# The first block of every other AFNO chunk gets a buffer of its own, and its transfer out is issued in two parts

## The chip, the cores and the metric

The program runs on one core of one Trainium2 chip, as one launch. The metric is device time in microseconds (us), lower is better, given as the median of several runs. A hardware profile of one execution on the same core goes with it. In it PE is TensorE, DVE VectorE, ACT ScalarE, POOL GpSimd and SP SyncE, which here only issues transfers. PSUM is the memory that matmuls write to, SBUF the on-chip working memory; a transfer is a DMA, and it "lands" when its semaphore tells that all of its data has arrived.

## The reference, cut to what matters

One row of conditioning `c` gives six vectors (shift, scale and gate for each of two sublayers). The first sublayer is a spectral block (AFNO) on a sequence of 4096 rows of 640 columns, the second a gated feed-forward block.

```python
mod = (_silu(c) @ w_mod).reshape(c.shape[0], 6, 1, -1)
sa, ca, ga, sb, cb, gb = (mod[:, 0], mod[:, 1], mod[:, 2], mod[:, 3], mod[:, 4], mod[:, 5])
h = _layernorm(x) * (1 + ca) + sa
x = x + ga * _A_ref(h, A_w1, A_b1, A_w2, A_b2)     # spectral block
h = _layernorm(x) * (1 + cb) + sb
x = x + gb * _B_ref(h, B_w_gate, B_w_up, B_w_down) # silu(h Wg) * (h Wu) Wd, F = 1728

# _A_ref: rfft over the rows, then per frequency and per block of 160 of the 640 columns:
hr = relu(zr @ w1[0] - zi @ w1[1] + b1[0]);  hi = relu(zi @ w1[0] + zr @ w1[1] + b1[1])
or_ = hr @ w2[0] - hi @ w2[1] + b2[0];       oi_ = hi @ w2[0] + hr @ w2[1] + b2[1]
# soft threshold: sign(v) * max(|v| - 0.01, 0) for or_ and oi_, then irfft
```

## The kernel before, in words

The program has three parts. A first stage normalizes `x`, takes a short Fourier transform along one factor of the row index and writes the result to scratch memory. The AFNO loop, which the change touches, does the rest of the forward transform, the two small layers, the soft threshold and the first half of the inverse transform. The feed-forward part ends the inverse transform and does the second sublayer; its instructions are put in order by a planner in the code, and the change does not touch it.

**The AFNO loop.** The frequencies are done in 8 chunks (`ch`) of 256 (258 in chunk 4), the 640 columns in 4 blocks (`b`) of 160. One step `p = 4 * ch + b` is one chunk and one block. The loop over `p` writes all engines' instructions in this order, and each engine runs its own in that order (the scheduler is off there). A step is software-pipelined: step `p` does layer 1 of block `p` (`stage_l1`), the transform of a later chunk's columns (`stage_b`, `evac_b`, `evac_rh`, `evac_rl`), layer 2 of block `p - 1` (`stage_l2`), the inverse transform of a piece that is seven steps old (`stage_i`), and, between them, pieces of the soft threshold (`shrink_parts`, `shrink`, `shrink_high`, `shrink_low`).

**Where layer 2 goes.** `stage_l2` makes, for each half `q` of the chunk's 256 frequencies, a PSUM tile `pc` of 128 frequencies by 2 x 160 values (real, imaginary). DVE adds the bias (L731) and writes the result into columns `160 * b` of a tile `tt` of 128 x 2 x 640. There are two `tt` buffers in all, one for each `q`. So block 0 of a chunk writes into the buffers that still hold the chunk before.

**The moves.** After the last block of chunk `ch - 1` is written, at the end of step `p = 4 * ch`, `move_x` puts eight transfers on the SP queue (L745): for each of four pieces `i` (quarters of the chunk's frequencies) two, one for the real and one for the imaginary half, from 64 partitions of `tt` into 64 partitions of a tile `xx` of 128 x 640. Block 0 of chunk `ch` is written in step `4 * ch + 1`; the semaphores make it wait until the moves that read its buffer have landed.

**The threshold.** ACT computes two relus of `xx` (`shrink_parts`, L751 into `cl`, L752 in place) in step `4 * ch + 1 + i` for piece `i` of chunk `ch - 1`, behind that step's layer-1 evacuations; DVE subtracts them at the start of the next step (L757). Then ACT and DVE split the result in a high and a low part (L766, L771) for the inverse matmuls `pi` (L782 to L784), which ACT evacuates (L785). In step `p` ACT's queue goes on, behind `shrink_parts`, with the next step's evacuations of layer 1 (`h`, L682 and L683; `u` first part, L696), and DVE's with the second part of `u` (L697). The second `pi` of a step takes the PSUM buffer that `u` was evacuated from.

**The conditioning vectors.** Beside this, four of the six vectors are computed on DVE, 20 rows of `w_mod` in 20 steps: `mod_load` fetches 128 x 640 numbers into the tile `wm` through the SP queue (L553), and `mod_add` multiplies and adds them into `acc` (L558 for the first of a vector, L560 for the others). `wm` has one buffer, so a load waits for the `mod_add` before it. In the steps that write block 0, a `mod_add` stands right behind the two bias additions (step 5) or behind one L771 more (steps 9, 13, 21, 25).

**What sets the order.** SP issues its transfers strictly in the order written, each after the semaphores that it waits for; a transfer also waits for the one eight transfers before it, since eight semaphores are used in turn. Nothing else is issued on SP while one waits.

At the end of the loop the first rows of the feed-forward part are prepared in three tiles, of which the third takes the place of `wm` (line 1009), and the feed-forward part begins with loads `cr` (L1504) of the AFNO result.

Of the kernel before, what the change touches and what calls it, by code (L numbers as in the profile page):

```python
# [13 lines left out]
P = 128  # L14
D = 640
# [158 lines left out]
def body(tc, x, w1, b1, w2, b2, wg, wu, wd, c, wm, k_fa, k_tb, k_tx, k_bm, k_bx, k_ga, k_ge, k_id, out, dbg=None):  # L174
# [27 lines left out]
    with ExitStack() as top:  # L202
# [35 lines left out]
        with ExitStack() as af:  # L238
# [292 lines left out]

            acc = p2.tile([P, D], F32, name="acc")
# [16 lines left out]
            wmts = {}  # L549

            def mod_load(m, k):
                wmts[m, k] = p2.tile([P, D], F32, tag="wm", bufs=1, name=f"wm{m}_{k}")
                nc.sync.dma_start(wmts[m, k], wm[:, m, k, :])  # L553

            def mod_add(m, k):
                wmt = wmts[m, k]
                if k == 0:
                    dve.tensor_scalar(acc, wmt, sc[:, 0:1], None, op0=OP.mult)  # L558
                else:
                    dve.scalar_tensor_tensor(acc, wmt, sc[:, k:k + 1], acc, op0=OP.mult, op1=OP.add)  # L560
                if (m, k) == (0, 4):
                    remainders(acc, wx)
# [44 lines left out]
            tts = {}  # L607

# [104 lines left out]
            def stage_l2(ch, b, then=()):  # L713
                h0, h1, r2, _ = hss[ch, b]
                de = slice(160 * b, 160 * b + 160)
                for q in range(3 if ch == CE else 2):
# [3 lines left out]
                    if b == 0 and q < 2:  # L720
                        tts[ch, q] = p2.tile([P, 2, D], F32, tag="tt", bufs=2, name=f"tt{ch}_{q}")
# [8 lines left out]
                    if q < 2:  # L730
                        dve.tensor_tensor(tts[ch, q][:, :, de], pc[:, :320].rearrange("p (r e) -> p r e", r=2),  # L731
                                          b2t[:, :, b, :], op=OP.add)
                        if then:
                            then[q]()
                    else:

                        dve.tensor_tensor(tts[ch, 0][0:1, 1, de], pc[0:1, :160], b2t[0:1, 0, b, :], op=OP.add)
# [3 lines left out]
            def move_x(ch, i):  # L741
                q, h = i // 2, i % 2
                xx = p2.tile([P, D], F32, tag="xx", bufs=5, name=f"xx{ch}_{i}")
                for r in range(2):
                    nc.sync.dma_start(xx[64 * r:64 * r + 64, :], tts[ch, q][64 * h:64 * h + 64, r, :])  # L745
                xxs[ch, i] = xx

# [100 lines left out]
            for p in range(LAST + 1):  # L848
# [35 lines left out]
                if b == 0 and ch:  # L884
                    for i in range(4):
                        move_x(ch - 1, i)
                if p == 0:
# [9 lines left out]
                for f, *a in mods.get(p, ()):  # L897
                    f(*a)
                if p == LAST - 4:
# [108 lines left out]
            for i in range(3):  # L1008
                xns[0].append(p2.tile([P, D], F32, tag="co" if i < 2 else "wm", bufs=2 if i < 2 else 1, name=f"xn0_{i}"))
# [1202 lines left out]
```

## Time and profile before

| | us |
|---|---|
| median of 3 runs | 1473.19 (1470.07 to 1473.38) |
| time of the profiled execution | 1472.98 |
| span of the profiled execution | 1471.2 |
| AFNO loop, first layer-2 result to the last `xx` move | 72.9 to about 277 |
| DVE's waits for the moves before it writes `tt` | 12.0 in 6 waits |
| mean granted clock of PE | 0.991 |

A row of the chain or of the groups names the engine, the line of the code, the operation and the tiles (out<-in). In a timeline row the first number is the start in us from the span's start, the second the duration, and what stands in brackets is the idle time just before the row and the instruction that ended it. A row `PE pi L782 <- DVE u L697: 1.9, 2, 1.2` of the table of waits says that PE, before line 782, stood idle for 1.9 us in 2 waits, the longest 1.2, and that line 697 on DVE ended them. Matmul busy time is pipelined time, so PE at 97% does not mean that PE is at its peak; it does mean that there is little room between matmuls.

### The profile page before, as it was taken

Reading aid. Unit: us, or ns where it says so; the run is one execution under the profiler, and the core shown is the slowest. Engines: PE = TensorE matmul, PEld = TensorE weight load, DVE = VectorE, ACT = ScalarE, POOL = GpSimd, SP = SyncE. Lnnn points to the kernel's source line nnn. Section 1 sums busy time; section 2 is a strip of 40 time slices with the busy share of each in tenths; the row PEclk is TensorE's granted clock in tenths of the full one; section 3 lists DMA queues with packets and bytes.
Section 4 is the critical chain, followed back from the end, with each engine's and each line's share of the span. In section 5 each row is a group of like instructions: output and inputs, shape, how many; then the busy total and the mean of one; then the engine's idle time right before and its main releaser. Section 6 shows DMA issues by size and latency. Waiting matters only on the chain.

```text
span 1471.2 us, 23664 instructions
## 1 busy us (share of the span) xinstructions
PE 1432.1 (97%) x8656; PEld 1353.6 (92%) x8656; DVE 1054.7 (72%) x1901; ACT 781.7 (53%) x1517; POOL 413.4 (28%) x529
## 2 busy tenths in 40 slices
PE   8899999989999999999999999999999999999999
PEld 4699999858878888899999999999999999999998
DVE  8968888877787787657777767787656566466653
ACT  7779989744445455435554545545453344344331
POOL 4500200055544344312433322433411121111111
PEclk9999999989999999999999999999999999999999
DMA  9956566656777986796775995776884345944422
GB/s 361 326 198 205 162 184 210 204 177 224 235 263 241 337 280 206 263 370 197 235 245 191 334 353 181 248 231 215 324 290 137 120 149 195 355 135 144 143 76 83
DMA packets 155927, 332.06 MB, mean 226 GB/s; under 512 B 19873, under 2 KB 79073, under 8 KB 154018
## 3 DMA queue, kind: packets, MB, share of 16 engines
q1 hardware_dynamic: 147426, 313.99, 63.1%
q0 software_dynamic: 6800, 13.93, 2.9%
q10 hardware_dynamic: 1584, 2.62, 0.5%
q8 instruction: 68, 1.11, 0.3%
q14 instruction: 49, 0.40, 0.1%
HBM read 234.35 MB, written 86.64 MB: 218 GB/s over the span
## 4 chain that ended last, share of the span: by engine, by line
PE 69%; issue 9%; DVE 9%; DMA 8%; ACT 3%; POOL 2%; SPq 1%; POOLq 0%; DVEq 0%; ACTq 0%
PE pd L2085 23%; PE pw L1890 8%; PE pw L1892 7%; PE pw L1891 7%; PE pg L1813 3%; PE pg L1814 3%; PE pg L1815 3%; PE pw L1901 2%; PE pw L1903 2%; PE pw L1902 2%; DMA cr<-s 2%; DVE st_a L193 2%; PE py L1533 1%; DMA wt<-td 1%; DVE wb L1347 1%
## 5 line engine op out<-in xcount | busy, mean ns | idle before, releaser
L2085 PE MATMUL pd<-wdh,a 128*128 128x320 f32 x1672 | 381.3, 310 | 1.5 <-DVE x L2057 1.1
L2085 PEld LDWEIGHTS pd<-wdh,a 128*128 128x128 f32 x1672 | 283.0, 188 | 2.5 <-DVE x L2057 1.4
L2085 PE MATMUL pd<-wdl,a 128*128 128x320 f32 x868 | 267.3, 309 | 0.0
L2057 DVE TENSOR_TENSOR x<-x,pd 128x320 f32<-128x320 f32 x384 | 178.2, 481 | 93.9 <-PE pd L2085 90.7
L1347 DVE TENSOR_TENSOR wb<-r,wb 128x512 fp32r<-128x512 f32 (+3 forms) x170 | 167.8, 994 | 16.1 <-ACT wb L1340 15.0
L2085 PEld LDWEIGHTS pd<-wdl,a 128*128 128x128 f32 x868 | 163.1, 188 | 0.5
L1890 PE MATMUL pw<-h,wt 128*128 128x384 f32 x416 | 141.6, 340 | 5.0 <-DMA wt<-td 2.9
L1444 ACT ACTIVATE wdh<-wdr 128x640 fp32r<-128x640 f32 x84 | 60.9, 733 | 149.8 <-PE pd L2085 142.2
L1892 PE MATMUL pw<-h,wt 128*128 128x384 f32 x416 | 140.2, 337 | 0.0
L1891 PE MATMUL pw<-h,wt 128*128 128x384 f32 x416 | 140.0, 337 | 0.0
L1340 ACT ACTIVATE wb<-r 128x768 fp32r<-128x768 f32 (+3 forms) x168 | 115.3, 701 | 20.3 <-PE pg L1815 11.7
L1934 POOL TENSOR_TENSOR sg<-s_x,sg 128x384 f32<-128x384 f32 x24 | 26.4, 1101 | 339.1 <-DVE s_x L1916 304.6
L1890 PE MATMUL pw<-h,wb 128*128 128x384 f32 x312 | 105.0, 337 | 0.0
L1892 PE MATMUL pw<-h,wb 128*128 128x384 f32 x312 | 104.6, 335 | 0.0
L1891 PE MATMUL pw<-h,wb 128*128 128x384 f32 x312 | 104.6, 335 | 0.0
L1937 DVE TENSOR_TENSOR a<-sg,a 128x384 fp32r<-128x384 f32 x104 | 80.2, 775 | 32.9 <-ACT a L1936 32.6
L1813 PE MATMUL pg<-ht,wb 128*128 128x512 f32 x260 | 103.7, 399 | 0.0
L1814 PE MATMUL pg<-ht,wb 128*128 128x512 f32 x260 | 102.0, 392 | 0.0
L1815 PE MATMUL pg<-ht,wb 128*128 128x512 f32 x260 | 101.6, 391 | 0.0
L1448 DVE TENSOR_TENSOR wdl<-wdr,wdh 128x640 fp32r<-128x640 f32 x84 | 74.6, 898 | 27.2 <-ACT wdh L1444 27.1
L1890 PEld LDWEIGHTS pw<-h,wt 128*128 128x128 f32 x416 | 78.6, 189 | 7.8 <-DMA wt<-td 3.5
L1516 POOL TENSOR_TENSOR cr<-cr,gab 128x640 f32<-128x640 f32 x28 | 48.2, 1720 | 119.3 <-DMA cr<-s 116.4
(278 smaller groups left out, 3380.7 us busy)
## 6 DMA issues: line engine op xcount, KB each, us to landing
wt<-td SPq DMA_DIRECT2D x104, 512.0 KB, 5.2
hs<-ho SPq DMA_DIRECT2D x52, 512.0 KB, 5.1
h<-hs SPq DMA_DIRECT2D x32, 768.0 KB, 9.9
r<-in_B_w_up_dram SPq DMA_DIRECT2D x36, 640.0 KB, 5.7
r<-in_B_w_gate_dram SPq DMA_DIRECT2D x36, 640.0 KB, 5.1
wdr<-wdd SPq DMA_DIRECT2D x35, 640.0 KB, 4.1
td<-wt SPq DMA_DIRECT2D x25, 512.0 KB, 4.7
xx<-tt SPq DMA_DIRECT2D x56, 160.0 KB, 3.8
```

Of the source, the lines that this page charges most:

```text
L1340: def high(ks, e=slice(0, c), copy=lambda o, i: act.activation(o, i, AF.Copy)):
L1347: dve.tensor_tensor(wbs[t, n][:, 1, ks, e], raw[t, n][:, ks, e], f32(wbs[t, n][:, 0, ks, e]), op=OP.subtract)
L1448: dve.tensor_tensor(l[:, f], wdraw[t, p][:, f], f32(h[:, f]), op=OP.subtract)
L1813: mm(b, wh, hh, start=(kk == 0), stop=False)
L1814: mm(b, wh, hl, start=False, stop=False)
L1815: mm(b, wl, hh, start=False, stop=(kk == 4))
L1890: mm(b, w(0, kp), a[:, kp, 0], start=start and kp == 0, stop=False, skip_group_check=not start)
L1891: mm(b, w(0, kp), a[:, kp, 1], start=False, stop=False, skip_group_check=not start)
L1892: mm(b, w(1, kp), a[:, kp, 0], start=False, stop=kp == 1, skip_group_check=not start)
L1937: Step("V", cv_ + 0.1, lambda: dve.tensor_tensor(o[:, 1], sg, f32(o[:, 0]), op=OP.subtract), (("ah", key),), ("act", t, fc, a), free=("sg" ...
L2057: dve.tensor_tensor(x2[:, e], x2[:, e], x[0][:, :320], op=OP.add)
L2085: mm(pd[g, hf][0][:, :320], l, m, start=i == 0, stop=i == len(s) - 1 and not (last and len(gs) > 1))
```

## The change

In chunks 1, 3 and 5, block 0 is no longer written into `tt`. Its two results (`q` = 0 and 1) go into two new tiles `te` of 128 x 2 x 160 (two buffers, one for each `q`), and the `tt` buffers are taken only from block 1 on. Chunks 0, 2, 4, 6 and 7 write block 0 into `tt` as before.

The moves of chunks 1, 3 and 5 are split: `move_x` takes columns 160 to 639 (64 partitions by 480 columns), and a new function `move_first` takes the 160 columns of block 0 from `te`, two transfers for each piece `i`. The transfers of `move_first` for piece 0 are issued right behind the eight of `move_x`, ahead of the loads and the `mod_load` of that step, and those for pieces 1 to 3 behind them. For the other chunks `move_first` issues nothing. So 24 transfers are added, all on SP, in steps 8, 16 and 24.

The tile `wm`, until now allocated anew for each load, becomes one tile `wmt` that is allocated first in its pool; the third prepared row tile at the end of the loop takes it over. This shifts the places of the tiles in SBUF. In the feed-forward part the order of all engines is the same; the first `cr` load now also waits for the transposes of that third tile (L1752) and its normalization (L1013), since it lies where that tile was.

```diff
--- before.py
+++ after.py
@@ -529,6 +529,7 @@
             nc.sync.dma_start(tx, k_tx)
             p2 = af.enter_context(tc.tile_pool(name="p2", bufs=1, side="right", reuse_waits="tile"))
 
+            wmt = p2.tile([P, D], F32, name="wm")
             acc = p2.tile([P, D], F32, name="acc")
             cl = p2.tile([P, D], F32, name="cl")
             wx = p2.tile([P, P], F32, name="wx")
@@ -546,14 +547,10 @@
 
 
             nc.sync.dma_start(bx.rearrange("p a b -> p (a b)"), k_bx)
-            wmts = {}
-
             def mod_load(m, k):
-                wmts[m, k] = p2.tile([P, D], F32, tag="wm", bufs=1, name=f"wm{m}_{k}")
-                nc.sync.dma_start(wmts[m, k], wm[:, m, k, :])
+                nc.sync.dma_start(wmt, wm[:, m, k, :])
 
             def mod_add(m, k):
-                wmt = wmts[m, k]
                 if k == 0:
                     dve.tensor_scalar(acc, wmt, sc[:, 0:1], None, op0=OP.mult)
                 else:
@@ -605,6 +602,7 @@
             rzs = {}
             hss = {}
             tts = {}
+            ttx = {}
 
             def width(ch):
                 return 258 if ch == CE else 256
@@ -717,7 +715,9 @@
                     fs = slice(128 * q, 128 * q + 128) if q < 2 else slice(256, 258)
                     M = 128 if q < 2 else 2
                     W = 320 if q < 2 else 160
-                    if b == 0 and q < 2:
+                    if b == 0 and q < 2 and ch % 2 and ch < NCH - 1:
+                        ttx[ch, q] = p2.tile([P, 2, 160], F32, tag="te", bufs=2, name=f"te{ch}_{q}")
+                    if b == ((ch, 0) in ttx) and q < 2:
                         tts[ch, q] = p2.tile([P, 2, D], F32, tag="tt", bufs=2, name=f"tt{ch}_{q}")
                     pc = ps.tile([P, 512], F32, tag="p2" if q < 2 else "p1", name=f"pc{ch}_{b}_{q}")
                     seq = [(h0[:, 0, fs], w2a[:, b, 0:W]), (h0[:, 1, fs], w2a[:, b, 0:W]),
@@ -728,7 +728,8 @@
                     for i, (l, m) in enumerate(seq):
                         mm(pc[:M, :W], l, m, start=(i == 0), stop=(i == len(seq) - 1))
                     if q < 2:
-                        dve.tensor_tensor(tts[ch, q][:, :, de], pc[:, :320].rearrange("p (r e) -> p r e", r=2),
+                        to = ttx[ch, q] if b == 0 and (ch, q) in ttx else tts[ch, q][:, :, de]
+                        dve.tensor_tensor(to, pc[:, :320].rearrange("p (r e) -> p r e", r=2),
                                           b2t[:, :, b, :], op=OP.add)
                         if then:
                             then[q]()
@@ -741,9 +742,17 @@
             def move_x(ch, i):
                 q, h = i // 2, i % 2
                 xx = p2.tile([P, D], F32, tag="xx", bufs=5, name=f"xx{ch}_{i}")
+                k = slice(64 * h, 64 * h + 64)
+                lo = 160 * ((ch, q) in ttx)
                 for r in range(2):
-                    nc.sync.dma_start(xx[64 * r:64 * r + 64, :], tts[ch, q][64 * h:64 * h + 64, r, :])
+                    nc.sync.dma_start(xx[64 * r:64 * r + 64, lo:], tts[ch, q][k, r, lo:])
                 xxs[ch, i] = xx
+
+
+            def move_first(ch, i):
+                q, h = i // 2, i % 2
+                for r in range(2 if (ch, q) in ttx else 0):
+                    nc.sync.dma_start(xxs[ch, i][64 * r:64 * r + 64, :160], ttx[ch, q][64 * h:64 * h + 64, r, :])
 
 
             def shrink_parts(ch, i):
@@ -884,6 +893,8 @@
                 if b == 0 and ch:
                     for i in range(4):
                         move_x(ch - 1, i)
+                    for i in range(1):
+                        move_first(ch - 1, i)
                 if p == 0:
                     for n in (3, 4):
                         weights_high(*prep2[n])
@@ -896,6 +907,9 @@
                     load_tb(ch + 2)
                 for f, *a in mods.get(p, ()):
                     f(*a)
+                if b == 0 and ch:
+                    for i in range(1, 4):
+                        move_first(ch - 1, i)
                 if p == LAST - 4:
                     cf += [rp.tile([P, 2, D], F32, tag=tag, name=f"cf{tag}") for tag in ("rm", "rr")]
                     load_first_rows(rb + 16, rl, nc.sync)
@@ -1006,7 +1020,7 @@
                     fst.append((mv, rs, nm))
 
             for i in range(3):
-                xns[0].append(p2.tile([P, D], F32, tag="co" if i < 2 else "wm", bufs=2 if i < 2 else 1, name=f"xn0_{i}"))
+                xns[0].append(p2.tile([P, D], F32, tag="co", bufs=2, name=f"xn0_{i}") if i < 2 else wmt)
 
             def first_norm(i):
                 _, rs, nm = fst[i]
```

The first place is the SP queue from the moves of chunk 1 (step 8) on. `xx_0` to `xx_3` are the four pieces, `wm` the rows of `w_mod`, `g` and `tb` the inputs of a later chunk; `x2` stands for two transfers. Before:

```order
L745 DMA xx_0_1432<-tt_0_1131 64x640 x2
L745 DMA xx_1_1435<-tt_0_1131 64x640 x2
L745 DMA xx_2_1438<-tt_1_1142 64x640 x2
L745 DMA xx_3_1441<-tt_1_1142 64x640 x2
L553 DMA wm_4_1445<-in_w_mod_dram 128x640
L553 DMA wm_0_1641<-in_w_mod_dram 128x640
L313 DMA g_1742<-s 128x1x2560
L299 DMA tb_1744<-in_k_tb_dram 128x512
```

In the changed program (L748 is `move_x`, L755 `move_first`, L551 `mod_load`):

```order
L748 DMA xx_0_1431<-tt_0_1214 64x480 x2
L748 DMA xx_1_1434<-tt_0_1214 64x480 x2
L748 DMA xx_2_1437<-tt_1_1225 64x480 x2
L748 DMA xx_3_1440<-tt_1_1225 64x480 x2
L755 DMA xx_0_1431<-te_0_1131 64x160 x2
L551 DMA wm<-in_w_mod_dram 128x640
L755 DMA xx_1_1434<-te_0_1131 64x160 x2
L755 DMA xx_2_1437<-te_1_1142 64x160 x2
L755 DMA xx_3_1440<-te_1_1142 64x160 x2
L551 DMA wm<-in_w_mod_dram 128x640
L313 DMA g_1747<-s 128x1x2560
L299 DMA tb_1749<-in_k_tb_dram 128x512
```

The load of `wm` that stood right behind the eight moves now stands behind ten transfers, and the transfers for `xx_1` to `xx_3` stand between it and the next `wm` load, with `g` and `tb` behind all of them.

The second place is DVE where block 0 of chunk 1 is written (step 5). `pc_0_0` and `pc_0_1` are the PSUM tiles of layer 2, `b2t` the bias. Before:

```order
L731 TENSOR_TENSOR tt_0_1131<-pc_0_0_1132,b2t 128x2x160
L731 TENSOR_TENSOR tt_1_1142<-pc_0_1_1143,b2t 128x2x160
L558 TENSOR_SCALAR acc<-wm_0_1070,sc 128x640
L757 TENSOR_TENSOR xx_0_1058<-cl,xx_0_1058 128x640
L684 TENSOR_TENSOR h_2_0_1169<-h_1_2_0_1168,h_2_0_1169 128x256
```

In the changed program (L732 is the bias addition, L555 the first `mod_add` of a vector, L766 the subtraction of the threshold, L682 the low part of `h`):

```order
L732 TENSOR_TENSOR te_0_1131<-pc_0_0_1132,b2t 128x320
L732 TENSOR_TENSOR te_1_1142<-pc_0_1_1143,b2t 128x320
L555 TENSOR_SCALAR acc<-wm,sc 128x640
L766 TENSOR_TENSOR xx_0_1059<-cl,xx_0_1059 128x640
L682 TENSOR_TENSOR h_2_0_1168<-h_1_2_0_1167,h_2_0_1168 128x256
```

Nothing moves on DVE; only the target of the two bias additions changes, and `mod_add` still stands right behind them.

## The prediction

> **What bounds the kernel.** First the page: the busy row and the chain that ended last.
>
> ```profile
> PE 1432.1 (97%) x8656; PEld 1353.6 (92%) x8656; DVE 1054.7 (72%) x1901; ACT 781.7 (53%) x1517; POOL 413.4 (28%) x529
> ...
> PE 69%; issue 9%; DVE 9%; DMA 8%; ACT 3%; POOL 2%; SPq 1%; POOLq 0%; DVEq 0%; ACTq 0%
> ```
>
> PE sets the end. So a wait elsewhere is worth only the idle time of PE that it causes. I therefore read next who held PE in the AFNO loop (94 to 300 us), and set it beside DVE's waits for the moves there.
>
> ```profile
> PE pi L783 <- DVE xl L771: 2.1, 2, 1.1
> PE pi L782 <- DVE u L697: 1.9, 2, 1.2
> PE pl L679 <- DVE tt L737: 1.8, 1, 1.8
> PE pi L836 <- ACT co L785: 1.2, 1, 1.2
> PE pc L729 <- DVE tt L731: 0.4, 1, 0.4
> PE pm L575 <- DVE acc L560: 0.3, 1, 0.3
> PE pm L570 <- DVE acc L560: 0.3, 1, 0.3
> PE pi L782 <- ACT xh L766: 0.3, 1, 0.3
> ```
>
> ```profile
> DVE tt L731 <- DMA xx<-tt: 12.0, 6, 2.7
> ```
>
> DVE waits 12.0 us for the moves, but PE is idle for 8.3 us in the whole loop (the sum of the eight rows), and most of that is at other places. The gain on offer is far below 12.
>
> **Part 1: the waits that go (chunks 1, 3, 5).** Block 0 of these chunks no longer waits for the moves. Chunk 1 on DVE, and then PE's idle time behind it:
>
> ```profile
> 100.14 0.49 DVE L731 TENSOR_TENSOR tt<-pc,b2t 128x320 f32<-128x320 f32 x1
> 103.36 0.49 DVE L731 TENSOR_TENSOR tt<-pc,b2t 128x320 f32<-128x320 f32 x1 [2.73 <-DMA xx<-tt]
> 104.06 0.55 DVE L558 TENSOR_SCALAR acc<-wm,sc 128x640 f32<-128x640 f32 x1 [0.20 <-DMA wm<-in_w_mod_dram]
> ```
>
> ```profile
> 109.09 0.71 PE L729 MATMUL pc<-w2a,h 128*128 128x320 f32 x3 [0.36 <-DVE tt L731]
> ...
> 112.81 0.42 PE L782 MATMUL pi<-xh,bm 128*128 128x320 f32 x1 [0.65 <-DVE u L697]
> ```
>
> The 2.73 us go, but the next instruction on DVE is the multiply of `w_mod`, and it already waits for its own load until 104.06. That load stands behind the moves of chunk 0 on SP, which the change leaves alone. So the wait passes from one instruction to the next, and from 104.06 on nothing is earlier. I take 0; the other bound is all of PE's idle time behind it, 0.36 + 0.65 = 1.0 us off. For chunks 3 and 5 the table of PE's waits has no row that their waits could have caused but the 0.3 of L570: I take 0, bound 0.3 off.
>
> **Part 2: a new wait of ACT (steps 9, 17, 25).** Piece 0 of chunks 1, 3 and 5 is complete only when its two `te` transfers have landed. They are issued as ninth and tenth, and so in the place where the `wm` load now stands:
>
> ```profile
> 128.16 0.53 SPq L553 DMA_DIRECT2D wm<-in_w_mod_dram  x1
> ```
>
> ```profile
> 186.68 0.58 SPq L553 DMA_DIRECT2D wm<-in_w_mod_dram  x1
> ```
>
> ```profile
> 247.89 0.52 SPq L553 DMA_DIRECT2D wm<-in_w_mod_dram  x1
> ```
>
> An issue takes 0.59 us here, and the times from issue to landing are these, for the moves (first two rows) and the `wm` loads (last):
>
> ```profile
> L745 SPq DMA_DIRECT2D xx<-tt x56: 469/590/1893, 94.2 to 276.3; - x56
> ...
> DMA to landing us min/median/max: 2.6/3.8/5.7
> ```
>
> ```profile
> DMA to landing us min/median/max: 2.9/3.0/4.3
> ```
>
> No row shows 64 rows of 160 numbers (40 KB). I bound its landing by 2.6 and 3.8, least and median of the moves of 160 KB, and take 3.0: the `wm` median for 320 KB that mostly go alone, while these follow eight moves that now carry a quarter less. The second `te` transfer is issued 0.59 behind each of the three times above, so it lands at 131.75, 190.27 and 251.48.
>
> Chunk 2, first ACT, then DVE, then PE:
>
> ```profile
> 128.24 0.82 ACT L751 ACTIVATE cl<-xx,nlam 128x640 f32<-128x640 f32 x1
> ...
> 131.40 0.38 ACT L696 ACTIVATE u<-pl 64x256 f32<-64x256 f32 x1
> ```
>
> ```profile
> 132.03 0.88 DVE L560 SCALAR_TENSOR_TENSOR acc<-wm,sc,acc 128x640 f32<-128x640 f32 x1 [0.15 <-DMA wm<-in_w_mod_dram]
> ...
> 134.50 0.47 DVE L697 SCALAR_TENSOR_TENSOR u<-pl,b1r,u 64x256 f32<-64x256 f32 x1
> ```
>
> ```profile
> 135.02 0.41 PE L782 MATMUL pi<-xh,bm 128*128 128x320 f32 x1 [1.24 <-DVE u L697]
> ```
>
> ACT starts L751 at 131.75 instead of 128.24, 3.5 us late. L696 then ends at 131.78 + 3.5 = 135.3, and L697, which reads its result, starts there instead of at 134.50: 0.8 late. The second way is longer: the `wm` load is issued two places later (2 x 0.59 = 1.18), L560 had waited for its landing, and DVE has no gap from there to L697: 1.2 late. PE already waits for L697 and passes this on in full: **+1.2**. With 2.6 the `wm` way still gives 1.2; with 3.8 ACT is 4.3 late, L697 1.6.
>
> Chunk 4, ACT and PE:
>
> ```profile
> 188.85 0.82 ACT L751 ACTIVATE cl<-xx,nlam 128x640 f32<-128x640 f32 x1
> ...
> 192.55 0.48 ACT L682 ACTIVATE h<-pl,b1m 128x258 f32<-128x258 f32 x1 [1.29 <-PE pl L679]
> ```
>
> ```profile
> 191.28 0.63 PE L679 MATMUL pl<-z,w1a 128*128 128x258 f32 x3 [1.85 <-DVE tt L737]
> ```
>
> PE's 1.85 belong to chunk 4's own wait for the moves, which stays. ACT is 190.27 - 188.85 = 1.42 late and had 1.29 idle: **+0.1** (0 with 2.6; 2.22 - 1.29 = 0.9 with 3.8).
>
> Chunk 6, ACT, DVE, PE:
>
> ```profile
> 249.03 0.82 ACT L751 ACTIVATE cl<-xx,nlam 128x640 f32<-128x640 f32 x1
> ...
> 254.59 0.42 ACT L704 ACTIVATE r<-u 64x256 fp32r<-64x256 f32 x1 [0.32 <-DVE u L697]
> ...
> 259.49 0.38 ACT L696 ACTIVATE u<-pl 64x256 f32<-64x256 f32 x1
> ```
>
> ```profile
> 260.45 0.47 DVE L697 SCALAR_TENSOR_TENSOR u<-pl,b1r,u 64x256 f32<-64x256 f32 x1
> ...
> 264.61 0.88 DVE L560 SCALAR_TENSOR_TENSOR acc<-wm,sc,acc 128x640 f32<-128x640 f32 x1
> ```
>
> ```profile
> 265.64 1.25 PE L575 MATMUL pm<-ones,acc 128*128 128x1 f32 x10 [0.34 <-DVE acc L560]
> ```
>
> ACT is 2.45 late, less the 0.32 that it had idle: 2.13, and no other gap stands up to 259.49. L696 ends at 259.87 + 2.13 = 262.0, L697 starts there instead of at 260.45: 1.55 late. L560 follows it without a gap and PE waits for L560. So PE loses between L697's 1.55 and ACT's 2.13; I take **+1.9** (1.4 with 2.6; with 3.8 ACT 2.9 and L697 2.35, so 2.7).
>
> The `wm` load, too, is 1.18 later in both: it lands by 190.9 in chunk 4, ahead of its use behind the moves' wait, and by 252.1 in chunk 6, where DVE's other lag is the longer: 0.
>
> **Part 3: the rest of SP's queue.** Six more issues, 6 x 0.59 = 3.5 us, stand ahead of the next `wm`, `g` and `tb` in each of the three steps. `wm` for step 10 waits for a `mod_add` anyway, and `g` is read a chunk later: 0. Pieces 1 to 3 of `te` are needed one to three steps later: 0.
>
> **Part 4: the places in SBUF.** The first `cr` load newly waits for the transposes. They and the wait that it has:
>
> ```profile
> L1752 PE MATMUL pt<-idn,xn x20: 272/273/328, 320.3 to 322.8; 128*128 128x128 f32 x20
> ```
>
> ```profile
> SPq L1504 <- DMA s<-cz: 16.0, 1, 16.0
> ```
>
> ```profile
> 326.81 0.34 SPq L1504 DMA_DIRECT2D cr<-s  x1
> ```
>
> The transposes end by 323.1, the transfer that the load waits for at 326.8: hidden, 0; the cover is 3.7 us.
>
> **The sum.** 0 + 1.2 + 0.1 + 1.9 = +3.2 us. The profiled execution took 1472.98, 1.8 more than its span; it becomes 1476.2. The median is 0.2 above it: **1476.4**. Bounds: 1.2 + 0 + 1.4 - 1.0 - 0.3 = +1.3, and 1.6 + 0.9 + 2.7 = +5.2.
>
> [...]
>
> **Rivals.**
> - *`te` lands late* (slower). ACT's rows from 128 to 131 and 249 to 259 have almost no gap, so from some point each tenth of a microsecond reaches PE three times. With landings at the moves' maximum, 5.7, ACT's lag is 6.2, 4.1 and 5.1, and the terms are 3.5 + 2.8 + 4.5 = 10.8: 1484.0. It decides (over 4.4, which is 0.3%) from a landing of 3.55 on (1.4 + 0.7 + 2.4 = 4.5). For it: the moves' median is 3.8. Against: `wm`, with eight times a `te` transfer's bytes, has 3.0. Chance 0.34, mostly near the bound, about 1478.5.
> - *The waits count in full* (faster). If half of DVE's 12.0 us had held PE, -6.0: 1467.2. Against: the 1.0 us that PE lost behind chunk 1, and the `wm` load that ends at the same time. 0.08.
> - *Nothing happens*, since ACT comes to L751 after `te` has landed: 1473.2. In chunk 2 the second transfer is issued at 128.75, after ACT comes there (128.24); excluded there, 0.03 for the sum to be near nothing otherwise.
>
> **Numbers.** 0.3% (4.4 us) is about what a measurement can tell from no change. Likeliest, with its own range 1474.5 to 1477.6: 0.55. Same 0.55 + 0.03 = 0.58, slower 0.34, faster 0.08. The range of 8 in 10 goes from 1471.5, where the bound of chunk 1 and the lower runs lie, to 1481, half way into late landings.
>
> **What would show it.** Right: no wait of DVE at `te`, and 2.5 to 3.5 us of idle before `acc` in step 5 instead; about six of the 12.0 us left, in chunks 2, 4, 6 and 7; ACT idle before L760 (the old L751) for a transfer from `te`, some 3.5, 1.4 and 2.4 us; PE's wait for `u` in chunk 2 at 2.4 instead of 1.24. Wrong: `acc` in step 5 well ahead of 104, `te` landing beyond 3.6 us or before ACT arrives, or a change of more than 1 us in the feed-forward part.

## The result, and the profile after

The changed kernel takes 1474.74 us (median of 22 runs), the kernel before 1472.52 (22 runs beside them). The ratio is 1.0014, with a 95% interval from 1.0001 to 1.0027: +2.1 us, within the 0.3% that I called no change. The forecast was 1476.4. The profiled execution took 1477.88 us with a span of 1476.1, 4.9 more than that of before; it is one of the longer ones, 3.1 us above the median.

The sum came out near, but its terms did not, and the profile after shows that first. PE's waits in the AFNO loop (94 to 306 us), with the total, how often, and the longest (the rows for `u` and `tt`):

```profile
PE pi L791 <- DVE u L695: 5.0, 4, 2.1
...
PE pl L677 <- DVE tt L738: 1.1, 2, 0.7
```

PE waits more for `u` (1.9 us before), and less for `tt` (1.8 before). DVE's waits for transfers in the same stretch, then ACT's new one:

```profile
DVE acc L557 <- DMA wm<-in_w_mod_dram: 8.0, 5, 2.5
...
DVE acc L555 <- DMA wm<-in_w_mod_dram: 4.3, 2, 2.8
...
DVE tt L732 <- DMA xx<-tt: 3.3, 4, 1.2
```

```profile
ACT cl L760 <- DMA xx<-te: 3.9, 3, 1.7
```

The wait for the moves fell from 12.0 to 3.3 us, further than to the half that I had left standing. The moves (first row) land sooner than the 3.8 us of before, and the `te` transfers (second row) are these, from issue to landing:

```profile
DMA to landing us min/median/max: 2.2/3.0/5.0
```

```profile
DMA to landing us min/median/max: 1.9/2.4/3.9
```

ACT waits 3.9 us for `te`, not 7.4. The wait for `w_mod` grew from about 0.4 us to 12.3: that is where DVE now stands. Its places, from the timeline of DVE (start, duration, instruction, idle time before it):

```profile
104.60 0.55 DVE L555 TENSOR_SCALAR acc<-wm,sc 128x640 f32<-128x640 f32 x1 [2.77 <-DMA wm<-in_w_mod_dram]
...
133.29 0.89 DVE L557 SCALAR_TENSOR_TENSOR acc<-wm,sc,acc 128x640 f32<-128x640 f32 x1 [2.26 <-DMA wm<-in_w_mod_dram]
...
263.31 0.89 DVE L557 SCALAR_TENSOR_TENSOR acc<-wm,sc,acc 128x640 f32<-128x640 f32 x1 [2.55 <-DMA wm<-in_w_mod_dram]
```

And what PE makes of it (chunk 1, chunk 2, chunk 4, and step 27 in chunk 6), from its timeline:

```profile
113.36 0.41 PE L791 MATMUL pi<-xh,bm 128*128 128x320 f32 x1 [0.66 <-DVE u L695]
...
136.28 0.58 PE L791 MATMUL pi<-xh,bm 128*128 128x320 f32 x1 [1.95 <-DVE u L695]
...
192.49 0.63 PE L677 MATMUL pl<-z,w1a 128*128 128x258 f32 x3 [0.69 <-DVE tt L738]
...
266.04 0.63 PE L791 MATMUL pi<-xh,bm 128*128 128x320 f32 x1 [2.12 <-DVE u L695]
```

The gap of chunk 1 is the same as before (0.65). That of chunk 2 grew from 1.24 to 1.95, that of chunk 4 shrank from 1.85 to 0.69, and at 266 there is a new one of 2.12. It comes from SP's queue, which holds a `wm` load back (SP's timeline after, then the same load before):

```profile
250.86 0.53 SPq L551 DMA_DIRECT2D wm<-in_w_mod_dram  x1
251.44 4.66 SPq L755 DMA_DIRECT2D xx<-te  x6
256.46 0.55 SPq L852 DMA_DIRECT2D cfrm<-s  x1
257.11 0.54 SPq L852 DMA_DIRECT2D cfrr<-s  x1
257.74 0.54 SPq L551 DMA_DIRECT2D wm<-in_w_mod_dram  x1
```

```profile
252.79 0.35 SPq L553 DMA_DIRECT2D wm<-in_w_mod_dram  x1
```

The last of these loads is issued 5 us later than before, and its sum starts only at 263.31, 5.6 us behind the issue. Before, nobody waited for it.

For all runs below I use one length: from the start of the first `pi` matmul of the loop to that of the last, read from the group's row. Before it is 295.4 - 111.6 = 183.8 us, after 300.1 - 112.1 = 188.0:

```profile
L782 PE MATMUL pi<-xh,bm x56: 302/309/418, 111.6 to 295.4; 128*128 128x320 f32 x56
```

```profile
L791 PE MATMUL pi<-xh,bm x56: 303/309/633, 112.1 to 300.1; 128*128 128x320 f32 x56
```

So the loop takes 4.2 us more in the profiled execution. From there to the end the distance is the same as before, to 0.2 us. That is chance rather than a sign: no run below changes the instructions behind the loop, and in the profiled executions this part takes from 1166 (`wm` ahead of `te`) to 1176 us (changed kernel). A median time carries that spread; a loop length is free of it, but is one execution's.

One more thing differs from one execution to the next. In some stretches of 3.41 us the profile shows a granted clock of 0.50 (more under "The half clock"). In such a stretch behind a gap PE does 16 entries (changed kernel, from 136.37), where it did 31 in the kernel before (from 135.44), so I estimate that each one costs about half its length, 1.7 us. The table counts those inside the loop. Before has none, although its gap of 1.85 in chunk 4 is as long as some that have one behind them.

### The profile page after: what moved, and what is told of

It is laid out like the page before. It is cut to its first block, busy times and chain, and to the rows that moved or that the text cites. A ratio compares the mean times of both kernels' runs of the same rounds, so it can differ in the third digit from the quotient of the medians.

```text
span 1476.1 us, 23703 instructions
## 1 busy us (share of the span) xinstructions
PE 1436.2 (97%) x8656; PEld 1357.2 (92%) x8656; DVE 1053.6 (71%) x1901; ACT 781.2 (53%) x1517; POOL 415.5 (28%) x529
## 4 chain that ended last, share of the span: by engine, by line
PE 71%; issue 9%; DVE 8%; DMA 7%; ACT 3%; POOL 2%; SPq 1%; POOLq 0%; DVEq 0%; ACTq 0%
PE pd L2099 23%; PE pw L1904 8%; PE pw L1906 8%; PE pw L1905 8%; PE pg L1828 3%; PE pg L1827 3%; PE pg L1829 3%; PE pw L1917 2%; PE pw L1916 2%; PE pw L1915 2%; DMA cr<-s 2%; PE py L1547 1%; DVE st_a L193 1%; PE pl L677 1%; DVE wb L1361 1%
```

## The experiments

All twelve runs; the ratio is to the kernel before on the same chip, the loop is the length just defined. The last three columns are of one execution, the profiled one.

| run | ratio (95% interval) | loop, us | at half clock | DVE for moves / `wm`, ACT for `te`, us |
|---|---|---|---|---|
| before | 1 | 183.8 | 0 | 12.0 / 0.4 / - |
| changed kernel | 1.0014 (1.0001 to 1.0027) | 188.0 | 2 | 3.3 / 12.3 / 3.9 |
| `wm` ahead of `te` | 1.0037 (1.0023 to 1.0050) | 192.6 | 3 | 4.1 / 6.0 / 9.3 |
| pieces late | 0.9994 (0.9977 to 1.0010) | 186.3 | 1 | 2.6 / 10.5 / 6.0 |
| both of these | 1.0045 (1.0028 to 1.0062) | 191.6 | 1 | 2.8 / 5.4 / 10.6 |
| dummies on the kernel before | 1.0160 (1.0139 to 1.0181) | not read | not read | see text |
| `wm` late in the pool | 1.0125 (1.0092 to 1.0158) | not read | not read | see text |
| dummies, second form | 1.0061 (1.0041 to 1.0082) | 188.6 | 2 | 9.3 / 4.9 / - |
| PE kept busy in two gaps | 1.0014 (0.9997 to 1.0031) | 185.7 | 0 | 2.2 / 13.2 / 4.0 |
| spread loads, changed kernel | 1.0008 (0.9989 to 1.0028) | 183.1 | 0 | 1.6 / 4.3 / 3.3 |
| no pieces | 0.9965 (0.9948 to 0.9982) | 181.9 | 1 | 3.0 / 4.2 / - |
| spread loads, kernel before | 0.9995 (0.9972 to 1.0017) | 182.4 | 0 | 9.9 / none / - |
| spread loads and pieces late | 1.0012 (0.9995 to 1.0029) | 188.6 | 1 | 3.7 / 3.0 / 6.2 |
| `te` early | 0.9981 (0.9962 to 1.0000) | 181.3 | 0 | 4.0 / 6.0 / none |

My first theory, from the profile after, was that the late `wm` loads are the price (A); the rival was that ACT's wait for `te` is (B), as forecast.

### The `wm` load ahead of all `te` transfers

```diff
                     for i in range(4):
                         move_x(ch - 1, i)
-                    for i in range(1):
-                        move_first(ch - 1, i)
...
                 if b == 0 and ch:
-                    for i in range(1, 4):
+                    for i in range(4):
                         move_first(ch - 1, i)
```

> Edit: in steps 8, 16 and 24 the wm load is issued right behind the eight moves, and all eight te transfers behind it; the rest as in the changed kernel. Theory A (the late wm loads are what costs): the wait of acc in step 9 falls from 1.3 us or more to under 0.5, PE's idle time before the second pi of step 10 falls from 1.95 to 1.3 or less, no stretch at half clock follows it, and the ratio to before is about 1.000 (a gain of 1.5 to 2.5 us on the changed kernel). The wm load of step 25 still stands behind the te transfers, so PE's 2.1 us at 266 stay. Rival B (ACT's wait for te is what costs): the te transfers land 0.6 us later, ACT's waits grow from 3.9 to about 5.7 us in all, and the ratio is 1.002 to 1.003.

The first half of A held: DVE's wait for `wm` was halved. The rest fell: the ratio went up, and PE's gap in step 10 with it. The timelines of PE, SP, DVE and ACT in chunk 2:

```profile
138.02 0.64 PE L791 MATMUL pi<-xh,bm 128*128 128x320 f32 x1 [2.70 <-DVE u L695]
```

```profile
128.92 0.53 SPq L551 DMA_DIRECT2D wm<-in_w_mod_dram  x1
129.50 1.74 SPq L755 DMA_DIRECT2D xx<-te  x3
```

```profile
132.28 0.88 DVE L557 SCALAR_TENSOR_TENSOR acc<-wm,sc,acc 128x640 f32<-128x640 f32 x1 [0.30 <-DMA wm<-in_w_mod_dram]
```

```profile
133.90 0.83 ACT L760 ACTIVATE cl<-xx,nlam 128x640 f32<-128x640 f32 x1 [4.06 <-DMA xx<-te]
```

Piece 0's second `te` transfer is the second of the three, issued near 130.1; ACT starts at 133.90, so it took some 3.8 us. In the changed kernel the same transfer stands ahead of the load (rows of SP, then of ACT): issued near 128.55, ACT starts at 130.54, 2.0 us.

```profile
127.92 1.25 SPq L755 DMA_DIRECT2D xx<-te  x2
129.26 0.53 SPq L551 DMA_DIRECT2D wm<-in_w_mod_dram  x1
```

```profile
130.54 0.83 ACT L760 ACTIVATE cl<-xx,nlam 128x640 f32<-128x640 f32 x1 [1.66 <-DMA xx<-te]
```

So here 40 KB issued behind 320 KB landed only behind them: DVE has the load by 132.28, ACT the transfer at 133.90. B, too, had the price too low (9.3 us of waits, not 5.7).

### Pieces 1 to 3 one per step, and both edits together

```diff
-                if b == 0 and ch:
-                    for i in range(1, 4):
-                        move_first(ch - 1, i)
+                if b and ch and (ch - 1, 0) in ttx:
+                    move_first(ch - 1, b)
```

> Edit: the te transfers of pieces 1, 2 and 3 are issued one piece per step, in the three steps that follow, behind the wm load of the step; the two of piece 0 stay where the changed kernel has them. Theory A: the wm load of step 25 is issued at about 255 instead of 257.7, DVE's 2.5 us before acc in step 26 and PE's 2.1 us at 266 go, with the half clock behind them, 2 to 3.6 us in all; the gap of 1.95 in step 10 stays; ratio to before 0.999 to 1.0005. Rival B: ACT's waits for the te of piece 0 are unchanged (3.9 us), and so is the ratio, 1.001 to 1.002.

> Edit: both of the above: the wm load right behind the moves, then the two te transfers of piece 0, and those of pieces 1, 2 and 3 one piece per step behind the wm load. Theory A: both lateness terms go and what the shorter wait for the moves gave in chunk 4 (PE 1.85 to 0.69) is left: ratio 0.998 to 0.9995, about 1471. Rival B: ACT waits 5.7 us for te instead of 3.9, ratio 1.002 or more.

For the first of the two A's main point held. The `wm` load of step 25 is issued at 252.08 and `acc` finds it there at 257.53; the gap of 2.12 is gone, and the ratio is within the range that A gave:

```profile
252.08 0.35 SPq L551 DMA_DIRECT2D wm<-in_w_mod_dram  x1
```

```profile
251.16 0.89 DVE L557 SCALAR_TENSOR_TENSOR acc<-wm,sc,acc 128x640 f32<-128x640 f32 x1 [1.87 <-DMA wm<-in_w_mod_dram]
257.53 0.88 DVE L557 SCALAR_TENSOR_TENSOR acc<-wm,sc,acc 128x640 f32<-128x640 f32 x1
```

But the interval reaches B's range as well, and two details went against A: the gap of step 10 did not stay at 1.95 but grew to 2.53, and ACT's waits for `te` grew to 6.0 us, with a fourth one for piece 1 of chunk 5, which now stands behind a `wm` load.

Both edits together, B held: ACT waits 10.6 us for `te`, ratio 1.0045. So neither theory is the whole: two transfers compete for the place behind the moves. With `te` ahead DVE waits 12.3 us for `wm`, with `wm` ahead ACT waits 9.3 us for `te`.

### The price of the queue alone, and the place of `wm`

```diff
+            dm = p2.tile([P, 2, 160], F32, name="dm")
+            dn = p2.tile([P, 160], F32, name="dn")
+            pool.memset(dm, 0.0)
...
+                    nc.sync.dma_start(dn[64 * r:64 * r + 64, :], dm[64 * h:64 * h + 64, r, :])
```

> Edit to the kernel before: block 0 stays in tt and the moves stay whole, but in steps 8, 16 and 24 eight dummy transfers of the same size (64x160, from a tile of zeros into a tile that nobody reads) are issued in the places of the te transfers. Computes all that the kernel before computes. Theory A: the wm loads are as late as in the changed kernel (issued 1.2 later in steps 8, 16, 24, about 5 later in step 25), DVE's 12.0 us of waits for the moves stay, and the ratio is 1.0015 to 1.004. Rival B: nobody waits for the dummies, so the ratio is 1.000.

The time is far above both, and for another reason. Near 60 us PE stood still for 18.3 us, since the weights of layer 2 waited for transfers out of the first stage's tile (18.73 us of idle time of ACT before `w2a`). I take it that the two new tiles had moved `w2a` over it, in a kernel where `wm` lies late in the pool. The run says nothing of the queue, also because the dummies, which all write one tile, waited for each other (11 waits on SP, 9.6 us). But it pointed to a part that I had passed over: the changed kernel allocates `wm` first. Undoing that alone:

```diff
-            wmt = p2.tile([P, D], F32, name="wm")
...
+                wmts[m, k] = p2.tile([P, D], F32, tag="wm", bufs=1, name=f"wm{m}_{k}")
+                nc.sync.dma_start(wmts[m, k], wm[:, m, k, :])
```

> Edit: the changed kernel with the wm tile allocated late in the pool, as the kernel before has it, instead of first. Nothing else. Theory A (the place of wm is a needed part of the change): with te the pool is 2.5 KB larger, the first tile of the second layer's weights (w2a) then lies over the tile that the spectrum of the first stage is written out from, and has to wait for these transfers; PE stands still for about 18 us near 60 us, as in the run with the dummy transfers, and the time is about 1493, ratio 1.012 to 1.016. Rival B (the place is worth nothing, as forecast in part 4): ratio 1.0014, as the changed kernel.

A holds, by two runs: 1489.32 us, and in ACT's timeline and in PE's waits

```profile
75.29 0.74 ACT L283 ACTIVATE w2a<-rm 128x640 fp32r<-128x640 f32 x1 [17.21 <-DMA s<-xa]
```

```profile
PE pl L680 <- ACT h L684: 16.8, 1, 16.8
```

Against the changed kernel that is 1.1%, 16 us, for the place of one tile. (No run has the new place of `wm` without `te`, so what the place alone does in the loop is not known.) Then the dummies again, eight in each of the three steps, on the changed kernel's layout:

```diff
-                    if b == 0 and q < 2 and ch % 2 and ch < NCH - 1:
+                    if False:
...
-                    nc.sync.dma_start(xxs[ch, i][64 * r:64 * r + 64, :160], ttx[ch, q][64 * h:64 * h + 64, r, :])
+                    nc.sync.dma_start(dn[64 * r:64 * r + 64, i, :], b2t[64 * h:64 * h + 64, r, 0, :])
```

> Edit to the changed kernel: block 0 of all chunks is written to tt and the moves are whole, as in the kernel before; the te transfers are replaced by eight dummies of the same size in the same places, each from a bias tile into its own part of a tile that nobody reads, so that no dummy waits for another. Computes all that the reference asks. It shows the price of the longer SP queue alone. Theory A: wm is as late as in the changed kernel (PE gaps of about 1.9 in step 10 and 2.1 in step 27), DVE's waits for the moves stay near 12 us and PE's 1.85 in chunk 4 too: ratio 1.002 to 1.004, above the changed kernel's 1.0014. Rival B: the dummies cost nothing since no engine waits for them: 1.000.

B is refuted. The ratio is above A's range, but not all of it is the queue's: PE waits 2.9 us for a `tt` between 40 and 95 us, ahead of the first dummy, where the changed kernel has no such wait, and the loop starts 5 us late (116.7 for 111.6). That leaves 4 of the 9 us by the times. Inside the loop it is 188.6 - 183.8 = 4.8 us, with these gaps of PE in steps 10 and 27, as A said, and that of chunk 4 between them:

```profile
140.83 0.41 PE L792 MATMUL pi<-xh,bm 128*128 128x320 f32 x1 [1.90 <-DVE u L695]
...
197.00 0.62 PE L677 MATMUL pl<-z,w1a 128*128 128x258 f32 x3 [1.95 <-DVE tt L738]
...
271.45 0.42 PE L792 MATMUL pi<-xh,bm 128*128 128x320 f32 x1 [1.85 <-DVE u L695]
```

But the two stretches at half clock in this loop stand behind 197.00 and 271.45, and the first of these gaps, for the moves, is in the kernel before too, where it has no such stretch behind it. Without that one, by the estimate of 1.7, the 24 transfers that nobody waits for cost about 3 us in the loop, by what stands behind them on SP.

### What the waits are worth without the price

```diff
-                for r in range(2 if (ch, q) in ttx else 0):
-                    nc.sync.dma_start(xxs[ch, i][64 * r:64 * r + 64, :160], ttx[ch, q][64 * h:64 * h + 64, r, :])
+                if (ch, q) in ttx:
+                    pool.memset(xxs[ch, i][:, :160], 0.0)
```

> Edit to the changed kernel: the 24 te transfers are left out; GpSimd writes zeros into their place in xx instead, so block 0 of chunks 1, 3 and 5 is left out of the computation (its layer 2 and its bias are still computed and written to te). It shows what the waits that go are worth with no price: eight shorter moves and nothing behind them. Theory A (part 1 of the forecast: the wait in chunk 1 passes to acc, which waits for wm): PE's 0.36 + 0.65 in chunk 1 stay, and what is gained comes from the shorter moves in chunks 2, 4 and 6 (PE's 1.85 in chunk 4 to 0.7 or less, 1.24 in step 10 to about 0.5): ratio 0.9975 to 0.9995. Rival B: the removed waits count for about half of DVE's 12 us: 0.996 or below.

The ratio is 0.9965, -5.2 us, between the two ranges, with an interval that reaches into both. The place of the gain is A's: chunk 1 keeps its two gaps, 1.24 in step 10 has no row here, and of the 1.85 in chunk 4 there is 0.46 left. PE's timeline and the loop:

```profile
109.05 0.71 PE L729 MATMUL pc<-w2a,h 128*128 128x320 f32 x3 [0.36 <-DVE tt L732]
...
112.77 0.42 PE L791 MATMUL pi<-xh,bm 128*128 128x320 f32 x1 [0.67 <-DVE u L695]
...
187.88 0.62 PE L677 MATMUL pl<-z,w1a 128*128 128x258 f32 x3 [0.46 <-DVE tt L738]
```

```profile
L791 PE MATMUL pi<-xh,bm x56: 303/309/417, 111.5 to 293.4; 128*128 128x320 f32 x56
```

The loop is 1.9 us shorter than before and 6.1 shorter than in the changed kernel (188.0 - 181.9). By the ratios the two kernels are 0.49% or 7.2 us apart, which the two intervals leave open by about 3 us either way. So the 24 transfers cost 6 to 7 us as measured, half-clock stretches included. The gain itself is less sure than the price: the profiled execution is 7.3 us shorter than that of before, but only 1.9 of this is in the loop (3.6 without its one stretch at half clock, by the estimate), and 5.3 lie behind the loop, where nothing was changed.

### The `wm` loads in other steps

```diff
-                for k in range(5):
-                    mods.setdefault(4 + 6 * i + k, []).append((mod_load, m, k))
-                    mods.setdefault(5 + 6 * i + k, []).append((mod_add, m, k))
+                for k, p in enumerate(((2, 3, 5, 6, 7), (9, 10, 11, 12, 13), (15, 17, 18, 19, 20), (21, 22, 23, 25, 26))[i]):
+                    mods.setdefault(p, []).append((mod_load, m, k))
+                    mods.setdefault(p + 1, []).insert(0, (mod_add, m, k))
```

(The lines that place `mod_sum` change with it.)

> Edit to the changed kernel: the wm loads are spread over other steps, so that none is issued in steps 4, 8, 16 and 24, where the moves are (loads in steps 2, 3, 5, 6, 7; 9 to 13; 15, 17 to 20; 21, 22, 23, 25, 26; the sums two steps earlier or as before). Theory A (the lateness of wm is what PE pays in chunk 2, and what hides the gain in chunk 1): DVE's waits for wm fall from 12.3 us to under 5, PE's 0.36 + 0.65 in chunk 1 go, the gap of 1.95 in step 10 falls to about 0.3 to 0.6, and the ratio is 0.997 to 0.9995. The load of step 25 still stands behind six te transfers, so the gap of 2.1 may stay. Rival B (ACT's wait for te carries the cost): gaps and ratio as in the changed kernel, 1.001 to 1.002.

> Edit to the kernel before: the wm loads in the other steps (as in the run with the spread loads: 2, 3, 5, 6, 7; 9 to 13; 15, 17 to 20; 21, 22, 23, 25, 26), nothing else. Theory A (te and the free wm are worth something only together): DVE's 12 us of waits for the moves stay, so chunk 1 keeps its 0.36 + 0.65 and chunk 4 its 1.85, step 10's 1.24 falls to about 0.5: ratio 0.9990 to 1.0003. Rival B (the spread loads alone are the gain, te adds none): chunk 1's gap goes here as well and the ratio is 0.9985 or below.

> Edit to the changed kernel: the spread wm loads and the te transfers of pieces 1 to 3 one piece per step behind them, both. Theory A (both late loads taken away, only ACT's wait for the te of piece 0 is left): no gap of 1.95 in step 10, none over 1 us at 260 to 266, ratio 0.996 to 0.9985, below both kernels. Rival B (ACT's wait for te, 3 to 6 us in all, now ends last and costs as much): 0.9994 or more, as the run with late pieces alone.

The first shows A's mechanism: PE's timeline has no wait from 94 to 150 us, and in chunk 1 DVE's two additions for block 0 (into `te`) and the two for block 1 (into `tt`) each run without a wait (timeline of DVE):

```profile
100.36 0.89 DVE L732 TENSOR_TENSOR te<-pc,b2t 128x320 f32<-128x320 f32 x2
106.27 0.89 DVE L732 TENSOR_TENSOR tt<-pc,b2t 128x320 f32<-128x320 f32 x2
```

The loop is 4.9 us shorter than in the changed kernel, which has two stretches at half clock more. The time does not confirm it: 1.0008, above A's range, with an interval that leaves both open. On the kernel before, the same table leaves the waits for the moves (9.9 us) and chunk 4's gap of 2.0, as A said; its loop is 1.4 us shorter, and the time undecided (0.9995). With the pieces late as well, B held, at 1.0012: ACT waited 3.49 us for `te` in chunk 4 and PE twice for `tt`, 3.4 us in all. The eight moves ahead of them took 6.9 us to issue there, against 5.3 in the changed kernel; why was not followed up. A fourth wait came from piece 1 of chunk 5, which now stands behind `wm`.

### The half clock

```diff
+                    for _ in range(9 if hf == 0 and (ch, i) in ((0, 3), (5, 0)) else 0):
+                        mm(pi[:, :320], bm[:, kd, 0, :], xh[:, e], start=True, stop=True)
```

> Edit to the changed kernel: in steps 10 and 27 the first of the matmuls of the first half of pi is issued nine times more (same operands, same bank, its result is overwritten by the real group), so that PE works for about 1.3 of the 1.95 and 2.12 us that it stood idle there. The result is unchanged. Theory A (the half clock behind these gaps costs): no stretch at half clock behind steps 10 and 27, matmuls of three take 0.52 instead of 0.84 us there, and the time is 1.5 us lower for each that is avoided: ratio 0.9995 to 1.0005. Rival B: the half clock is made good by waits later, or the nine matmuls delay the copy of pi: 1.0014 or more.

In the profile of the changed kernel the granted clock falls to 0.50 behind the gaps of 1.95 and 2.12 us. Here are the stretches with the gap and behind it (in each: length, busy times, the clock, DMA share, GB/s):

```profile
132.95:136.37 3.42, 1.48 (x11) 1.21 (x9) 3.05 (x7) 2.85 (x8) 0.00 (x0) 1.00 0.49 129
136.37:139.78 3.41, 3.41 (x16) 3.41 (x17) 3.30 (x7) 3.35 (x7) 0.54 (x1) 0.50 0.97 388
262.66:266.07 3.41, 1.29 (x10) 1.03 (x8) 2.76 (x6) 1.71 (x5) 0.00 (x0) 1.00 0.98 402
266.07:269.49 3.42, 3.42 (x15) 3.42 (x16) 3.31 (x7) 3.36 (x7) 0.54 (x1) 0.50 0.54 180
```

PE does 16 entries where the kernel before did 31 behind its 1.24 us of idle time:

```profile
135.44:138.85 3.41, 3.41 (x31) 3.41 (x31) 3.30 (x8) 3.35 (x7) 0.54 (x1) 1.00 0.90 370
```

With PE kept busy, groups of three matmuls behind the gap take 0.52 us, as in the kernel before, and not 0.84 as in the changed kernel:

```profile
136.80 0.41 PE L793 MATMUL pi<-xh,bm 128*128 128x320 f32 x1 [1.13 <-DVE u L695]
...
137.70 0.52 PE L677 MATMUL pl<-z,w1b 128*128 128x256 f32 x3
```

The loop is 2.3 us shorter than in the changed kernel. But the time is the same, 1.0014. So A is shown for the profiled execution and not for the runs. The interval (0.9997 to 1.0031) leaves room for a gain of 1.5 us, and what the added matmuls cost was not separated from what they save.

All runs together say more. Over the 95 executions of the kernel before beside the experiments (four chips), a mean granted clock lower by 0.001 goes with about 1.3 us more time, and one stretch of 3.41 us at 0.50 lowers the mean over the span by 0.0012. So these stretches go with a good part of the spread between executions of one kernel, which the changes in the loop have to be told from.

### `te` ahead of the moves

```diff
-                    for i in range(1):
-                        move_first(ch - 1, i)
...
-                if b == 0 and ch:
-                    for i in range(1, 4):
-                        move_first(ch - 1, i)
+                if p:
+                    move_first((p - 1) // 4, (p - 1) % 4)
```

Beside these lines, `move_first` and `move_x` now take the tile `xx` from one helper, which allocates it for whichever comes first. `te` is complete three steps before the moves; only the place in `xx` has to come free.

> Edit to the changed kernel: the te transfers of a chunk are issued before its moves instead of behind them: piece i's two at the end of the i-th step after the one in which te is written, behind the wm load of that step (each waits only until its part of xx is free); the last piece's two stand behind the moves and the wm load. Theory A (the whole price of te, about 7 us between the run without pieces, 0.9965, and the changed kernel, 1.0014, is the place of its transfers behind the moves): ACT does not wait for te, wm is as early as in the kernel before, PE has no gap over 1 us in steps 10, 18 and 27, and the ratio is 0.9955 to 0.9985, below both kernels. Rival B (24 more transfers cost SP and the DMA queues wherever they stand, or SP now waits for xx to come free and holds up wm): 0.9995 or more.

1468.17 us, ratio 0.9981, within A's range and 0.33% below the changed kernel, which is more than the two intervals leave open (about 0.23%). ACT has no wait for `te`. PE's waits, with the longest of chunk 4 at 1.0, and the loop, the shortest of all:

```profile
PE pi L795 <- DVE u L695: 1.1, 2, 0.7
PE pl L677 <- DVE tt L738: 1.0, 1, 1.0
PE pc L729 <- DVE tt L732: 0.4, 1, 0.4
```

```profile
L795 PE MATMUL pi<-xh,bm x56: 303/309/414, 112.8 to 294.1; 128*128 128x320 f32 x56
```

Against the kernel before it is -2.8 us, with an interval that ends at 1.0000 and so reaches B's range: below the changed kernel, but against the kernel before near to what can be told. By the loop nothing of the gain without pieces is missing (181.3 against 181.9, of which about 1.7 would be the one stretch at half clock), by the times 2.4 of the 5.2 us are; which of the two is right, the intervals do not tell.

## Why the forecast was near, point by point

- **Part 1, the waits that go: 0.** Right, and by its reason. Chunk 1's wait passed to `acc`, which then waited 2.77 us. Its two gaps stand in the run without pieces, where nothing else has changed there, and go when `wm` is not behind the moves (spread loads, changed kernel).
- **"PE's 1.85 belong to chunk 4's own wait for the moves, which stays."** This step failed. Chunk 4's block 0 waits for chunk 3's moves, and those are the ones that carry a quarter less. The median from issue to landing of all moves fell from 3.8 to 3.0 us, DVE's wait for them to 3.3 instead of "about six", and PE's gap to 0.69. Chunk 2 had the same gain in it. I counted the quarter only for the landing of `te`. The mechanism was left out of the sum; the run without pieces prices it, with part 1, at -5.2 us (-2.6 to -7.7) by the times and at -1.9 by the loop of one execution.
- **`te` lands 3.0 us after issue.** Mis-sized: about 2.0 for piece 0. ACT waits 1.7, 1.2 and 1.1, not 3.5, 1.4 and 2.4. Behind a `wm` load (run with `wm` ahead of `te`) it was 3.8.
- **Chunk 2, +1.2 by way of `wm`.** The way is right: DVE waits 2.26 us there and PE's gap grows. The size is 1.95 - 1.24 = 0.7. The load is issued 1.1 later (129.26 for 128.16), as I had it, but the whole step begins 0.5 later too (first move 122.35 for 121.81): the eight shorter moves take 5.5 us to issue instead of 6.3, so the load is only some 0.6 later within its step.
- **Chunk 6, +1.9 by way of ACT, and part 3, 0.** Both failed. ACT's lag was not the longer way. "`wm` for step 10 waits for a `mod_add` anyway" holds for step 10; I did not look at step 25, where the next load stands behind six issues and two loads of `cf` and is issued 5 us later. The late pieces undo it, and the ratio falls by 0.2%, about as much as the two intervals can tell.
- **Part 4, 0.** The time is right and the working missed the point. I priced the first `cr` load and did not ask why `wm` is allocated first; without that the change costs 18.6 us (1489.32 against 1470.73).
- **The sum.** +3.2 forecast, +2.1 measured. It is near by luck, because two errors cancel: a gain that I had at 0 (1.9 us by the loop, 5.2 by the times), and a price of 6.1 or 7.2 that I had at 3.2. And the loop of the profiled execution holds a term that I did not have at all: two stretches at half clock, about 3.4 of its 4.2 us by the estimate above.
- **The rivals.** "`te` lands late" did not happen in this kernel. Its price was about right where it was made to happen: landings of 3.8 us gave +5.4 us, where I had put the turn to slower at 3.55. "The waits count in full", -6.0, is near the -5.2 of the run without transfers, but not by its mechanism: chunk 1's wait went and PE's gaps behind it stayed.
- **What would show it.** The wait before `acc` in step 5 (2.77) is right. The feed-forward part is unchanged to 0.2 us, but as it varies by some 10 us between executions, this was no test. "About six of the 12.0", ACT's idle times and PE's 2.4 are wrong, each for the reason above.

What stays open is how much of the price is `wm` and how much is ACT. The dummies' 4.8 us in the loop without any wait for `te`, against 6.1 with it, would say that most is `wm`. But the dummies' loop holds two stretches at half clock where that of before holds none, and one of them stands behind a wait that is neither, so this does not settle it; the two were never late one without the other in the real kernel. What is shown is that the place of the `te` transfers behind the moves is the price, since the same transfers in earlier steps do not have it.

## What to carry to other kernels

Here the price of a transfer lay also in what stood behind it in its queue, into the next step, and not only in who reads it: three times eight small ones that nobody waited for made the loop 4.8 us longer, of which by the estimate about 3 are theirs. When two loads wanted the place behind a burst, moving one ahead of the other only changed who was late (waits of 12.3 us for `wm` and 3.9 for `te` became 6.0 and 9.3); moving one out of the burst altogether, to where its data is ready, took away most of the price (4.8 of 7.2 us by the times). And when the moves were split, the part that stayed was shorter (a median of 3.0 us to landing for 3.8), and here that gave the gain which the waits that went did not.

## What the runs showed of the chip that I had not expected

- **The half clock came in stretches of 3.41 us.** In the changed kernel a gap of 1.95 us lay in one such stretch, and the next one ran at 0.50. With both edits a gap of 2.74 us was cut in two by a border, and the clock stayed at 1.00 behind it (PE busy 2.19 and 1.90 in the two stretches):

```profile
132.14:135.56 3.42, 2.19 (x15) 1.93 (x14) 1.39 (x4) 2.57 (x5) 0.00 (x0) 1.00 0.66 157
135.56:138.97 3.41, 1.90 (x15) 1.90 (x16) 2.64 (x6) 3.30 (x8) 0.00 (x0) 1.00 0.88 342
138.97:142.38 3.41, 3.30 (x29) 3.09 (x28) 2.99 (x6) 3.35 (x8) 0.54 (x1) 1.00 0.52 194
```

  How much work in a stretch is enough, the runs do not tell: 1.60 us busy kept the clock with the pieces late, where 1.48 us did not in the changed kernel, but with the spread loads and late pieces it fell to 0.50 behind 1.67 us (from 197.19), and with the pieces late behind 2.68 us (from 265.48), of which 1.25 were ten matmuls of a single column. So busy time alone does not decide. In the changed kernel 1.9 and 2.1 us without work in one stretch were enough.
- **A small transfer behind a large one landed behind it**: 40 KB took 2.0 us behind moves and 3.8 behind a load of 320 KB that itself took some 3.4.
- **Two small tiles more in a pool cost 17 us of PE**: with `te` and `wm` late in the pool, ACT waited 17.21 us for transfers out of a tile of the first stage before it could write `w2a`, and PE 16.8 us behind it.
